# Blocks 2 to 6 are moved between quadrants inside SBUF, so that their sums run on 128x32 tiles

## The chip, the cores and the metric

The kernel runs on one core of a Trainium2 chip. The metric is device microseconds of one execution. Instructions stand in order on each of five engines: PE (matrix multiply), DVE (VectorE), ACT (ScalarE), POOL (GpSimd) and SP, which here only issues DMAs. SBUF has 128 rows (partitions); a quadrant is 32 of them. PE writes into PSUM, whose banks hold 128x512 floats.

## The reference, cut to what matters

```python
# attention between 512 tokens and 32 states, for 8 batches and 8 heads
xread = softmax(scale * x @ state.T) @ state
sread = softmax(scale * state @ x.T) @ x
x = concat([xread, sread], axis=2)              # 8 x (512 + 32) tokens of 512
h = x @ w_in                                    # 512 -> 2048, weights in float64
g = h / (1 + exp(-h))
y = g @ w_out                                   # 2048 -> 512
logits = y @ phi                                # 4352 tokens, 32 slots
d = softmax(logits, axis=tokens);  slot_input = d.T @ y
slot_out[e] = relu(slot_input[e] @ w1[e]) @ w2[e]    # 8 experts, 4 slots each
out = softmax(logits, axis=slots) @ slot_out
```

The kernel never forms y. It makes `w_out @ phi` once (tile `w2p`), takes the logits from g, and sums `d.T @ g` (32 slots by 2048 features) over all tokens. Only that sum is multiplied by w_out.

## The kernel before, in words

Eight blocks of 512 tokens (one batch each) are followed by a block 8 of the 256 state rows. Block k makes g in 16 steps j; step j = 4 fq + i holds features of quarter fq. A step is six full matmuls into a PSUM bank (`h`), an eviction on ACT (or tanh on ACT and a product on DVE for steps 2 to 5) into one of six rotating tiles `g`, and a DVE transpose of 32x32 squares from `g` into the buffer of the block, `blk` (two of these exist; 16x512 floats per partition). The logits (`lg`) of four steps follow as 128x32 matmuls. The weights of a quarter times the states (`wbp`, 64x32 tiles) are made one quarter ahead; their low part is a subtraction on DVE or POOL. Attention for blocks k+1 and k+2 (`sc`, `eT`, `sr`) is woven in.

In block k+1, `s_rep` makes the slot weights of block k: an exponential that writes them four times over (`d`), four PE transposes (`dT`) and one of the logits (`lT`). Then `s_dTg` sums. The DVE transpose works inside each quadrant, so quadrant q holds the tokens of its own 32 features of a step: the sum has to be made of 64 matmuls of 32x32, in four groups of 16 that run side by side, and every group adds to all four PSUM banks. Four DVE instructions then add the banks into `acc`. PE switches form (full, 64x32, 128x32, 32x32) between these kinds of work.

w_out comes as float64 bits in its own order too, half a quarter per block (`wo_block`, at step 10 of blocks 1 to 6, in the buffer of the next block): `conv_nat` makes float32 of it with one ACT and four DVE instructions, and it is stored to DRAM. The last two halves go through `wo_last`.

After block 7, `join7`, block 8 (`hid8`), `fold` (all of `acc` into one bank) and the slots' experts follow. w1 and w2, 32 loads of 1 MB, are loaded into places as these come free (`places`, `load_w`): quarters of the two block buffers, `acc`, the four tiles `win` of w_in, and others. Stores of the output end the program.

The order is not that of the code: a recorder notes each operation with its reads and writes, and a list scheduler picks for each engine the startable operation with the lowest number (place in the code, plus shifts, plus a table `RANK`). SP issues DMAs in one order, with at most eight under way.

Of the kernel before, what the change touches and what calls it, by code (L numbers as in the profile page):

```python
# [15 lines left out]
NB = 8  # L16
# [3 lines left out]
EPS = 1e-9  # L20
# [4 lines left out]
NAT = 10  # L25
# [3 lines left out]
RAW = [("win", 0), ("win", 1), ("wo", 0), ("win", 2), ("wo", 1), ("win", 3), ("wo", 2), ("wo", 3)]  # L29

# [37 lines left out]
    ("0", "ACT", "activation", "acc", 2): -44,  # L68
    ("0", "ACT", "activation", "acc", 3): -519,
    ("0", "ACT", "activation", "acc", 5): 1500,  # L70
    ("0", "ACT", "activation", "acc", 6): 1054,
    ("0", "ACT", "activation", "e", 1): 314,
    ("0", "ACT", "activation", "g", 2): 1009,
    ("0", "ACT", "activation", "g", 12): 347,
    ("0", "ACT", "activation", "part", 7): 723,
    ("0", "ACT", "activation", "s", 1): 373,
    ("0", "ACT", "activation", "win", 1): 190,
    ("0", "ACT", "activation", "win", 4): -1500,
    ("0", "ACT", "activation", "win", 5): -462,
    ("0", "ACT", "copy", "ws", 1): 1500,  # L80
    ("0", "ACT", "copy", "ws", 2): 1246,
    ("0", "DVE", "reduce_max", "asm", 0): -28,
    ("0", "DVE", "reduce_sum", "tm", 1): -405,
    ("0", "DVE", "tensor_scalar", "acc", 4): -317,
    ("0", "DVE", "tensor_scalar", "part", 3): -603,
    ("0", "DVE", "tensor_scalar", "tm", 2): -1193,
    ("0", "DVE", "tensor_scalar", "win", 0): -407,
    ("0", "DVE", "tensor_scalar", "win", 1): -38,
    ("0", "DVE", "tensor_scalar", "win", 4): 1334,
    ("0", "DVE", "tensor_scalar", "win", 5): -7,  # L90
    ("0", "DVE", "tensor_scalar", "win", 6): -1216,
    ("0", "DVE", "tensor_scalar", "win", 7): -1362,
    ("0", "DVE", "tensor_tensor", "s", 5): 1477,
    ("0", "DVE", "tensor_tensor", "wb", 2): 1151,
    ("0", "DVE", "tensor_tensor", "wb", 3): 574,
    ("0", "DVE", "transpose", "blk", 4): -1486,
    ("0", "DVE", "transpose", "blk", 13): 1451,
    ("0", "PE", "matmul", "sc", 2): 865,
    ("0", "PE", "matmul", "sr", 1): 590,
    ("0", "SP", "dma_start", "phi", 0): 1500,  # L100
    ("0", "SP", "dma_start", "raw", 0): 91,
    ("0", "SP", "dma_start", "raw", 2): 189,
    ("0", "SP", "dma_start", "raw", 3): 119,
    ("0", "SP", "dma_start", "raw", 4): 322,
    ("0", "SP", "dma_start", "raw", 5): -2,
    ("0", "SP", "dma_start", "raw", 6): 1174,
    ("0", "SP", "dma_start", "raw", 7): 1292,
    ("0", "SP", "dma_start", "xT", 0): -1080,
    ("0", "SP", "dma_start", "xT", 1): 1386,
    ("7", "ACT", "activation", "m", 0): 1500,  # L110
    ("7", "ACT", "copy", "rd", 0): -1500,
    ("7", "ACT", "copy", "wb", 3): 1125,
    ("7", "ACT", "copy", "wf", 1): 1156,
    ("7", "DVE", "scalar_tensor_tensor", "g", 1): 1500,
    ("7", "DVE", "tensor_scalar", "wo", 1): 1316,
    ("7", "DVE", "transpose", "blk", 2): 1500,
    ("7", "DVE", "transpose", "blk", 4): 1499,
    ("7", "PE", "matmul", "h", 8): 520,
    ("7", "PE", "matmul", "lg", 0): 1057,
    ("7", "PE", "matmul", "lg", 5): 74,  # L120
    ("7", "PE", "matmul", "lg", 12): 313,
    ("7", "PE", "matmul", "wbp", 1): 757,
    ("7", "PE", "transpose", "lT", 0): -377,
    ("8", "DVE", "tensor_copy", "place", 13): 166,
    ("8", "PE", "matmul", "S", 0): 823,
    ("8", "PE", "matmul", "f", 9): -334,
    ("8", "PE", "matmul", "f", 10): -1369,
    ("8", "PE", "matmul", "fold", 0): 1246,
    ("8", "PE", "matmul", "h", 6): -797,
    ("8", "PE", "matmul", "h", 13): 420,  # L130
    ("8", "PE", "matmul", "h", 29): 1217,
    ("8", "PE", "matmul", "lg", 4): 1500,
    ("8", "PE", "matmul", "o", 8): 984,
    ("8", "PE", "matmul", "o", 9): 1121,
    ("8", "PE", "transpose", "dT", 0): 788,
    ("8", "PE", "transpose", "gt", 5): 1212,
    ("m", "ACT", "activation", "e", 0): 695,
    ("m", "ACT", "activation", "e", 1): 1442,
    ("m", "ACT", "activation", "g", 11): -1243,
    ("m", "ACT", "activation", "s", 0): 1500,  # L140
    ("m", "ACT", "copy", "wb", 2): 1453,
    ("m", "ACT", "copy", "wf", 2): -422,
    ("m", "DVE", "reciprocal", "asm", 0): 1500,
    ("m", "DVE", "tensor_scalar", "asm", 0): 1500,
    ("m", "DVE", "tensor_scalar", "blk", 1): -1500,
    ("m", "DVE", "tensor_tensor", "blk", 0): 310,
    ("m", "DVE", "tensor_tensor", "wb", 3): 430,
    ("m", "PE", "matmul", "S", 0): 1500,
    ("m", "PE", "matmul", "h", 4): 505,
    ("m", "PE", "matmul", "h", 6): 1377,  # L150
    ("m", "PE", "matmul", "h", 9): 1448,
    ("m", "PE", "matmul", "lg", 0): 882,
    ("m", "PE", "matmul", "lg", 1): 935,
    ("m", "PE", "matmul", "lg", 4): 1040,
    ("m", "PE", "matmul", "lg", 9): 1500,
    ("m", "PE", "matmul", "sr", 0): 1500,
    ("m", "PE", "matmul", "wbp", 0): 371,
    ("m", "PE", "matmul", "wbp", 1): 775,
    ("m", "PE", "matmul", "wbp", 2): 1500,
    ("m", "PE", "transpose", "eT", 0): 1337,  # L160
# [8 lines left out]
def _runs(ap):  # L169


    dims = list(ap.ap)
    row = dims[0][0]
    if ap.space == bass.MemoryType.DRAM:
        return None
    p0, off = divmod(ap.offset, row) if row else (0, ap.offset)
    quads = 0
    for q in range(p0 // 32, (p0 + dims[0][1] - 1) // 32 + 1):
        quads |= 1 << q
    starts = [off]  # L180
    for step, count in dims[1:-1]:
        starts = [s + step * n for s in starts for n in range(count if step else 1)]
    step, count = dims[-1] if len(dims) > 1 else (1, 1)
# [12 lines left out]
    return quads, even, odd  # L196


class Recorder:
# [90 lines left out]
    def cost(self, op, eng, what, outs, ins, kwargs):  # L290
# [66 lines left out]
        else:  # L357
# [5 lines left out]
            op.cost = 0.42  # L363

# [217 lines left out]
def tile_state_attention_soft_moe(  # L582
# [95 lines left out]
    def conv_nat(raw, dst, pw):  # L678


        v = raw.rearrange("p (c f) b -> p c f b", f=dst.shape[-1])
        lo, hi, d = v[..., 0], v[..., 1], dst.bitcast(U32)
# [987 lines left out]
```

## Time and profile before

| | us |
|---|---|
| runs | 446.56, 447.78, 448.80; median 447.78 |
| the profiled execution | 448.13 |
| its span in the trace | 446.4 |
| PE busy | 420.8 (94%) |
| DVE, ACT, POOL busy | 320.9, 277.0, 99.3 |

The clock granted to PE is full until the last stretch. The span has a start that loads and converts weights (to some 97 us), blocks of 38.4 us each (to some 320 us), and the rest, in which w1 and w2 are loaded. S of block k stands in block k+1. A step's matmul leaves one record in the trace, a matmul in one of the smaller forms two, so that a group of four leaves 8; a few records are missing (a sum's 128 show as 121).

### The profile page before, as it was taken

What the parts mean: (1) busy time and instruction counts of PE and PEld (TensorE: products, weight loads), DVE (VectorE), ACT (ScalarE), POOL (GpSimd) and SP (SyncE); (2) the same over time, 40 slices, a digit from 0 to 9 for tenths busy, and PEclk for the clock granted to TensorE, in tenths of its full rate; (3) what the DMA queues carried; (4) which work ended last, traced back from release to release, by engine and by line L of the source; (5) the groups of instructions that cost most, each with busy time, mean ns of one, the idle gap of its engine ahead of it and who ended that gap; (6) DMA issues with size and microseconds to landing.
All of it is one profiled execution on the core that took longest, in us unless ns stands there. A gap on an engine that the chain in (4) does not pass through costs nothing.

```text
span 446.4 us, 11862 instructions
## 1 busy us (share of the span) xinstructions
PE 420.8 (94%) x5084; PEld 279.5 (63%) x5084; DVE 320.9 (72%) x566; ACT 277.0 (62%) x504; POOL 99.3 (22%) x63
## 2 busy tenths in 40 slices
PE   7889999999999999999999999999999998999970
PEld 5655565766766776676677667667677685334530
DVE  3989999788787976978788697879864654321460
ACT  4899996666775585686668568666746544111360
POOL 0024332152242413224142222421114220000000
PEclk9999999999999999999999999999999999999996
DMA  8999932323402602330370252125297889999997
GB/s 316 423 428 423 329 126 94 97 75 124 135 3 96 236 1 95 133 106 3 96 237 1 96 155 83 18 98 220 101 393 243 305 303 377 402 424 428 399 379 257
DMA packets 23205, 92.19 MB, mean 207 GB/s; under 512 B 1776, under 2 KB 10864, under 8 KB 14832
## 3 DMA queue, kind: packets, MB, share of 16 engines
q1 hardware_dynamic: 23152, 91.43, 55.0%
q8 instruction: 40, 0.66, 0.6%
q14 instruction: 13, 0.11, 0.1%
HBM read 79.37 MB, written 12.06 MB: 205 GB/s over the span
## 4 chain that ended last, share of the span: by engine, by line
PE 85%; DMA 6%; ACT 3%; DVE 2%; issue 1%; SPq 0%; DVEq 0%
PE h L543 43%; PE lg L543 8%; PE S L543 8%; PE wbp L543 6%; DMA xT<-in_xT_dram 5%; PE so L543 3%; PE f L543 3%; PE o L543 2%; PE sc L543 2%; PE eT L543 2%; PE sr L543 1%; DMA ss<-in_stT_dram 1%; DVE acc L543 1%; PE si L543 1%; PE gt L543 1%
## 5 line engine op out<-in xcount | busy, mean ns | idle before, releaser
L543 PE MATMUL h<-ar,wb 128*128 128x512 f32 x768 | 191.2, 401 | 2.7 <-ACT g L543 2.7
L543 PEld LDWEIGHTS h<-ar,wb 128*128 128x128 f32 x768 | 139.4, 188 | 51.7 <-issue 10.9
L543 DVE STREAM_TRANSPOSE blk<-g 128x512 f32<-128x512 f32 x128 | 88.7, 700 | 18.0 <-ACT g L543 17.4
L543 ACT ACTIVATE g<-h 128x512 f32<-128x512 f32 x100 | 59.0, 602 | 52.0 <-PE h L543 43.9
L543 POOL TENSOR_TENSOR wb<-wf,wb 128x512 fp32r<-128x512 f32 x26 | 34.7, 1333 | 83.2 <-PE lg L543 44.8
L543 POOL TENSOR_TENSOR s<-s,tm 128x1024 f32<-128x1024 f32 x12 | 23.3, 1940 | 91.9 <-DVE tm L543 90.3
L543 PE MATMUL S<-blk,dT 32*32 32x512 f32 (+1 forms) x1056 | 37.7, 591 | 0.0
L543 PEld LDWEIGHTS lg<-g,w2p 128*32 128x32 f32 x1056 | 26.9, 109 | 15.8 <-issue 11.5
L543 ACT CAST wb<-wbp 128x512 fp32r<-128x512 f32 x64 | 34.9, 607 | 3.0 <-PE wbp L543 3.0
L543 PE MATMUL lg<-g,w2p 128*32 128x128 f32 (+1 forms) x1056 | 36.6, 279 | 0.0
L543 PE MATMUL wbp<-win,ss 64*32 64x512 f32 x512 | 33.2, 596 | 0.4 <-DVE win L543 0.4
L543 DVE SCALAR_TENSOR_TENSOR acc<-acc,m,S 128x512 f32<-128x512 f32 x28 | 19.1, 743 | 12.3 <-PE S L543 12.3
L543 ACT ACT_TABLE_LOAD x21 | 26.9, 1283 | 1.1 <-PEq L1660 0.7
L543 DVE SCALAR_TENSOR_TENSOR g<-thb,h 128x512 f32<-128x512 f32 x28 | 18.6, 680 | 11.7 <-ACT thb L543 9.5
L543 PEld LDWEIGHTS S<-blk,dT 32*32 32x32 f32 (+1 forms) x1056 | 18.0, 103 | 13.8 <-issue 8.2
L543 DVE TENSOR_TENSOR wb<-wbp,wb 128x512 fp32r<-128x512 f32 x38 | 25.2, 676 | 1.7 <-ACT wb L543 1.4
L543 PE MATMUL h<-wc,rd 128*128 128x512 f32 x96 | 24.2, 402 | 0.0
L543 PE MATMUL lg<-thb 128*128 128x256 f32 x74 | 20.1, 415 | 1.2 <-DVE thb L543 1.2
L543 ACT COPY wf<-wbp 128x512 f32<-128x512 f32 x26 | 15.3, 588 | 7.9 <-PE wbp L543 5.6
L543 ACT ACTIVATE thb<-h 128x512 f32<-128x512 f32 x30 | 17.4, 595 | 4.1 <-PE h L543 3.8
L543 PEld LDWEIGHTS h<-wc,rd 128*128 128x128 f32 x96 | 17.4, 188 | 3.9 <-issue 0.2
L543 DVE TENSOR_REDUCE tm<-s 128x32 f32<-128x1024 f32 (+1 forms) x18 | 19.4, 1078 | 0.3 <-ACT s L543 0.3
(173 smaller groups left out, 576.2 us busy)
## 6 DMA issues: line engine op xcount, KB each, us to landing
place<-in_w_dram SPq DMA_DIRECT2D x17, 1024.0 KB, 7.5
blk<-in_w_dram SPq DMA_DIRECT2D x12, 1024.0 KB, 10.4
xT<-in_xT_dram SPq DMA_DIRECT2D x8, 1024.0 KB, 8.1
raw<-in_w_in_dram SPq DMA_DIRECT2D x8, 1024.0 KB, 14.0
raw<-in_w_outT_dram SPq DMA_DIRECT2D x8, 1024.0 KB, 8.1
xk<-in_xk_dram SPq DMA_DIRECT2D x8, 1024.0 KB, 4.8
blk<-in_w_out_dram SPq DMA_DIRECT2D x6, 1024.0 KB, 4.9
out_dram<-place SPq DMA_DIRECT2D x12, 512.0 KB, 7.7
```

What stands on the lines that cost most here:

```text
L543: made = [call(*args, **kwargs) for call, args, kwargs in op.calls]
```

## The change

The two block buffers get fixed names. `src` receives the transposes and `dst` is what the sum reads. For blocks 2 to 6 (`MOVED`) a quarter of features is moved by four DMAs from `src` to `dst`, inside SBUF: each reads 32 partitions of 8 KB and writes 128 partitions of 2 KB (256 KB), so that all 128 partitions hold tokens. There are 80 such DMAs, on SP. Quarter 0 of a block is moved after the sum of the block before; in blocks 3 to 6 `src` uses two quarters in turn, so the transposes of steps 8 to 11 write where quarter 0 lay. The sum of a moved block is 16 matmuls of 128x32, four per bank, and each bank is added to `acc` when its own four are done. The slot weights are written once, with one transpose, and their sum is multiplied by 4 with one small DVE instruction. Blocks 0, 1 and 7 keep the 32x32 form and write `acc` with a stride.

w_out in its own order goes through `conv`, as w_in does: two ACT instructions, one DVE shift and an integer add on POOL. It is done in the free part of `src`: two halves in block 1, then one each in blocks 3 to 6. `fold` is recorded right after the sum of block 7. Three of the `win` places are filled by four DMAs of 256 KB, each behind the part that it overwrites. The order table `RANK` is new throughout (three of its lines are shown).

```diff
-NAT = 10
+NATS = {1: {9: 0, 13: 1}, 3: {10: 2}, 4: {10: 3}, 5: {10: 4}, 6: {10: 5}}
...
+MOVED = (2, 3, 4, 5, 6)
...
-    ("8", "PE", "matmul", "S", 0): 823,
...
+    ("8", "PE", "matmul", "S", 0): 332,
...
+    ("m", "SP", "dma_start", "dst", 1): 754,
...
+            if outs[0].space == ins[0].space == bass.MemoryType.SB:
+                op.cost, op.bytes = 0.6, 1.5 * b
...
-    def conv_nat(raw, dst, pw):
...
-        nc.scalar.activation(out=dst, in_=hi.bitcast(F32), func=AF.Prelu, scale=2.0**-112, alpha=2.0**32)
-        nc.vector.tensor_scalar(
-            out=pw.bitcast(U32), in0=d, scalar1=3, scalar2=0xFF800000,
-            op0=ALU.logical_shift_left, op1=ALU.bitwise_and,
-        )
-        nc.vector.tensor_scalar(out=d, in0=d, scalar1=3, scalar2=None, op0=ALU.logical_shift_left)
-        nc.vector.scalar_tensor_tensor(out=pw, in0=lo, scalar=2.0**-52, in1=pw, op0=ALU.mult, op1=ALU.mult)
-        nc.vector.tensor_tensor(out=dst, in0=dst, in1=pw, op=ALU.add)
...
-        conv_nat(raw.rearrange("p (f b) -> p f b", b=2), dst, pw)
+        conv(raw.rearrange("p (f b) -> p f b", b=2), dst, pw, None)
...
+    LAST = ("dst", "src") if NB - 1 in MOVED else ("src", "dst")
...
+    def quarter(name, fq):
+        return bufs[name][:, 2048 * fq:2048 * fq + 2048]
+
+    def whole(k):
+
+        t = bufs["dst" if k == 1 else "src"]
+        if k == NB - 1:
+            return t.rearrange("p (y j t) -> p j y t", y=4, j=16)
+        return t.rearrange("p (j y t) -> p j y t", j=16, y=4)
+
+    def at_src(k, fq):
+        return quarter("src", fq if k == MOVED[0] else fq % 2)
+
+    def by_tokens(k, fq):
+
+        for q in range(4):
+            nc.sync.dma_start(
+                out=quarter("dst", fq)[:, 512 * q:512 * q + 512],
+                in_=at_src(k, fq)[32 * q:32 * q + 32].rearrange("r (x n) -> r x n", x=4),
+            )
...
-        if j == 0 and k not in blk_t:
-            new_blk(k)
-        nc.vector.transpose(out=blk_t[k][:, j], in_=g.rearrange("p (y t) -> p y t", y=4))
+        if j == 0 and k < 2:
+            new_blk(("src", "dst")[k])
+        if k in MOVED:
+            nc.vector.transpose(
+                out=at_src(k, fq).rearrange("p (t i c) -> p t i c", t=16, i=4)[:, :, i],
+                in_=g.rearrange("p (t r) -> p t r", t=16),
+            )
+            if i == 3 and fq:
+                by_tokens(k, fq)
+        else:
+            nc.vector.transpose(out=whole(k)[:, j], in_=g.rearrange("p (y t) -> p y t", y=4))
...
+        v = lg[:, 0:128].rearrange("p (y r) -> p y r", y=4)
+        if k in MOVED:
+            to = d = d[:, 0].rearrange("p q r -> p (q r)")
+            to = to.rearrange("p (r y) -> p y r", y=4)
+        else:
+            to, v = d, v.unsqueeze(2).to_broadcast(list(d.shape))
...
+        if k in MOVED:
+            nc.tensor.transpose(p[:, 0:128], d, ident)
+            nc.scalar.copy(out=dT[:, 0:128], in_=p[:, 0:128])
...
+            if k in MOVED:
+                nc.vector.tensor_scalar(out=m[:, 2:3], in0=m[:, 2:3], scalar1=4.0, scalar2=None, op0=ALU.mult)
...
+        def add(i):
+            o, v = acc[:, i], p[i]
+            if k not in MOVED:
+                o = acc.rearrange("p f (q n) -> p f q n", q=4)[:, :, i]
+                v = v.rearrange("p (f n) -> p f n", f=4)
+            if first:
+                nc.vector.tensor_copy(out=o, in_=v)
+            else:
+                nc.vector.scalar_tensor_tensor(out=o, in0=o, scalar=m[:, 3:4], in1=v, op0=ALU.mult, op1=ALU.add)
...
+        for fq in range(4):
+            v = quarter("dst", fq).rearrange("p (q n) -> p q n", q=4)
             with nc.together():
-                for q in range(4):
-                    for x in range(4):
+                for y in range(4):
+                    op = mm(
+                        p[fq][32 * y:32 * y + 32, :], lhsT=dT[:, 32 * y:32 * y + 32],
+                        rhs=v[:, :, 128 * y:128 * y + 128], start=True, stop=True,
+                    )
+            add(fq)
...
+    places = [(LAST[1], 2), (LAST[1], 3), "ss", "at", "A", ("w", 0), (LAST[0], 0), (LAST[0], 1), (LAST[0], 2), ("w", 1)]
+    places += ["g", ("w", 2), "acc", ("w", 3), "wb", "wb", "A", "x", (LAST[1], 0), (LAST[0], 3), "xT", "xk", "at", (LAST[1], 1)]
+    PIECES = (('w', 1), ('w', 2), ('w', 3))
...
+                if nxt_w[0] < len(places) and places[at_p] in PIECES:
+                    for x in range(4):
+                        nc.sync.dma_start(out=wt[kind, i][x], in_=src[:, 512 * x:512 * x + 512])
+                else:
+                    nc.sync.dma_start(out=t, in_=src)
...
                     s_dTg(k - 1)
+                    if k in MOVED:
+                        by_tokens(k, 0)
                     if k == NB - 1:
-                        new_blk(NB)
                         load_w(2)
...
-            if 1 <= k <= 6 and j == NAT:
-                wo_block(k - 1, k + 1)
+            if k in NATS and j in NATS[k]:
+                wo_block(NATS[k][j])
...
             s_dTg(NB - 1)
+            accX = fold()
...
-            accX = fold()
```

On PE, around the sum of block 3 (in block 4). Before (dT is the transposed slot weight, h4_7 step 7 of block 4, blk3 the buffer):

```order
L543 MATMUL dT3_417<-cst_66,d3_415 128x128 x4
...
L543 MATMUL h4_7_444<-ar4_374,wb17_420 128x512 x6
L543 MATMUL lg4_432<-g4_0_410,w2p_68 32x128 x4
...
L543 MATMUL lg4_432<-g4_4_429,w2p_68 32x128 x4
L543 MATMUL S3_0_0_439<-blk3_312,dT3_416 32x512 x4
L543 MATMUL S3_0_1_440<-blk3_312,dT3_416 32x512 x4
L543 MATMUL S3_1_0_441<-blk3_312,dT3_416 32x512 x4
L543 MATMUL S3_1_1_442<-blk3_312,dT3_416 32x512 x4
L543 MATMUL S3_0_0_439<-blk3_312,dT3_416 32x512 x4
...
L543 MATMUL S3_1_1_442<-blk3_312,dT3_416 32x512 x4
L543 MATMUL h4_8_447<-ar4_374,wb18_433 128x512 x6
```

After (dst the tokens of block 3, wbp19 the next weights):

```order
L579 MATMUL dT3_414<-cst_66,d3_412 128x128
...
L579 MATMUL lg4_429<-g4_4_426,w2p_68 32x128 x4
L579 MATMUL h4_6_434<-ar4_372,wb17_417 128x512 x6
L579 MATMUL h4_7_441<-ar4_372,wb17_417 128x512 x6
L579 MATMUL lT3_415<-cst_66,ls3_411 128x128
L579 MATMUL S3_0_0_436<-dst_186,dT3_413 32x512 x4
L579 MATMUL S3_0_1_437<-dst_186,dT3_413 32x512 x4
L579 MATMUL S3_1_0_438<-dst_186,dT3_413 32x512 x4
L579 MATMUL S3_1_1_439<-dst_186,dT3_413 32x512 x4
L579 MATMUL wbp19_0_0_450<-win3_81,ss_67 32x512 x4
L579 MATMUL wbp19_0_1_451<-win3_81,ss_67 32x512 x4
L579 MATMUL h4_8_444<-ar4_372,wb18_430 128x512 x6
```

The four groups of 16 became four groups of four, one to a bank. The logits stand before h4_6 instead of beside the sum, and wbp19 follows the sum.

On DVE, what follows the sum of block 3. Before:

```order
L543 STREAM_TRANSPOSE blk4_387<-g4_7_445 128x512
L543 SCALAR_TENSOR_TENSOR acc_69<-acc_69,m3_413,S3_0_0_439 128x512
L543 SCALAR_TENSOR_TENSOR acc_69<-acc_69,m3_413,S3_0_1_440 128x512
L543 SCALAR_TENSOR_TENSOR acc_69<-acc_69,m3_413,S3_1_0_441 128x512
L543 SCALAR_TENSOR_TENSOR acc_69<-acc_69,m3_413,S3_1_1_442 128x512
L543 STREAM_TRANSPOSE blk4_387<-g4_8_448 128x512
L543 STREAM_TRANSPOSE blk4_387<-g4_9_451 128x512
L543 TENSOR_SCALAR blk5_462<-blk5_462 128x1024
```

After (src is where quarter 0 of block 4 lay):

```order
L579 SCALAR_TENSOR_TENSOR acc_69<-acc_69,m3_410,S3_0_0_436 128x512
L579 SCALAR_TENSOR_TENSOR acc_69<-acc_69,m3_410,S3_0_1_437 128x512
L579 TENSOR_SCALAR tm5_400<-tm5_400 128x32
L579 STREAM_TRANSPOSE src_114<-g4_6_435 128x16x32
L579 SCALAR_TENSOR_TENSOR acc_69<-acc_69,m3_410,S3_1_0_438 128x512
L579 SCALAR_TENSOR_TENSOR acc_69<-acc_69,m3_410,S3_1_1_439 128x512
L579 TENSOR_TENSOR wb19_449<-wbp19_0_0_450,wb19_449 128x512
L579 STREAM_TRANSPOSE src_114<-g4_7_442 128x16x32
...
L579 STREAM_TRANSPOSE src_114<-g4_8_445 128x16x32
L579 STREAM_TRANSPOSE src_114<-g4_9_448 128x16x32
L579 STREAM_TRANSPOSE s5_398<-s5_398 128x1024
...
L579 TENSOR_TENSOR wb20_465<-wbp20_0_0_466,wb20_465 128x512
```

The transpose of g4_8, the first that overwrites quarter 0, stands behind the four adds and seven other instructions; behind it stand more transposes and the low part wb20.

On SP, from the load of batch 6's xT to that of batch 7 (xk is the other layout of x, wo_f32 the DRAM copy of w_out). Before:

```order
L543 DMA xT6_404<-in_xT_dram 128x2048
L543 DMA wo_f32_82<-blk4_387 128x1024
L543 DMA blk5_462<-in_w_out_dram 128x2x1024
L543 DMA xk6_459<-in_xk_dram 128x2048
L543 DMA xT7_479<-in_xT_dram 128x2048
```

After (dst from src are the moves):

```order
L579 DMA xT6_401<-in_xT_dram 128x2048
L579 DMA dst_186<-src_114 128x1x512 x4
L579 DMA src_114<-in_w_out_dram 128x2x1024
L579 DMA wo_f32_82<-src_114 128x1024
L579 DMA xk5_382<-in_xk_dram 128x2048
L579 DMA dst_186<-src_114 128x1x512 x2
L579 DMA wo_f32_82<-src_114 128x1024
L579 DMA dst_186<-src_114 128x1x512 x6
L579 DMA xT7_475<-in_xT_dram 128x2048
```

The loads of xk and xT, and the w_out stores, now stand between moves in the same queue.

## Rows read from the trace of the kernel before

**Rows 1.** The page: busy us (share of the span) and instructions of each engine.

```profile
PE 420.8 (94%) x5084; PEld 279.5 (63%) x5084; DVE 320.9 (72%) x566; ACT 277.0 (62%) x504; POOL 99.3 (22%) x63
```

**Rows 2.** Windows, two blocks: length, PE PEld DVE ACT POOL busy, clock, DMA, GB/s.

```profile
130.00:168.35 38.35, 38.35 (x521) 26.59 (x527) 31.23 (x54) 26.11 (x50) 11.35 (x8) 1.00 0.28 98
245.20:283.60 38.40, 38.40 (x524) 26.65 (x536) 31.18 (x54) 26.15 (x50) 11.40 (x8) 1.00 0.29 98
```

**Rows 3.** Chain of waits, one block: start us, us, engine, tile, instructions.

```profile
235.66 1.01 PE lg L543 x32
236.67 1.02 PE wbp L543 x16
237.69 2.96 PE h L543 x12
240.65 0.44 PE dT L543 x4
241.09 1.38 PE h L543 x6
242.47 0.11 PE lT L543
242.58 1.39 PE h L543 x6
243.97 1.23 PE lg L543 x40
245.20 4.39 PE S L543 x121
```

**Rows 4.** Chain of waits, an earlier block: what follows what.

```profile
138.20 2.77 PE h L543 x12
...
145.61 1.02 PE sc L543 x16
146.63 0.86 PE wbp L543 x16
```

**Rows 5.** Chain of waits after the blocks.

```profile
373.48 1.00 PE fold L543 x8
...
387.39 9.58 PE f L543 x88
...
397.55 1.85 PE f L543 x16
...
435.23 0.40 DVE place L543
```

**Rows 6.** DMA issues: KB each, median us from issue to landing.

```profile
raw<-in_w_in_dram SPq DMA_DIRECT2D x8, 1024.0 KB, 14.0
...
xk<-in_xk_dram SPq DMA_DIRECT2D x8, 1024.0 KB, 4.8
```

**Rows 7.** Groups of instructions: busy us, mean ns of one, idle before.

```profile
L543 DVE STREAM_TRANSPOSE blk<-g 128x512 f32<-128x512 f32 x128 | 88.7, 700 | 18.0 <-ACT g L543 17.4
...
L543 ACT ACTIVATE part<-raw,ulps 128x1024 uint32<-128x1024 uint32 x10 | 12.7, 1274 | 0.4 <-DMA raw<-in_w_in_dram 0.4
...
L543 DVE TENSOR_TENSOR blk<-blk 128x1024 f32<-128x1024 f32 x6 | 11.5, 1910 | 0.0
...
L543 POOL TENSOR_TENSOR acc<-acc,part 128x1024 uint32<-128x1024 uint32 x4 | 9.5, 2387 | 24.6 <-ACT part L543 16.4 <-DVE acc L543 8.2
```

**Rows 8.** Windows after the blocks, columns as before.

```profile
364.00:366.00 2.00, 2.00 (x12) 1.70 (x11) 1.38 (x2) 1.14 (x3) 0.00 (x0) 1.00 0.66 279
366.00:368.00 2.00, 2.00 (x10) 1.63 (x9) 0.00 (x0) 0.00 (x0) 0.00 (x0) 1.00 0.48 94
376.00:387.00 11.00, 9.30 (x143) 4.51 (x143) 5.69 (x23) 2.57 (x8) 0.00 (x0) 1.00 1.00 393
387.00:435.60 48.60, 44.92 (x552) 20.64 (x551) 17.70 (x45) 14.49 (x42) 0.00 (x0) 1.00 1.03 409
```

**Rows 9.** Chain of waits at the start.

```profile
12.80 21.07 DMA xT<-in_xT_dram
```

More of the change, by code (lines that the diff above doesn't have):

```diff
@@ L79 @@
[L79 to L89, printed above, removed]
@@ L101 @@
[L101 to L111, printed above, removed]
@@ L112 @@
[L112 to L123, printed above, removed]
@@ L136 @@
[L136 to L146, printed above, removed]
@@ L159 @@
-    ("m", "PE", "matmul", "wbp", 2): 1500,
-    ("m", "PE", "transpose", "eT", 0): 1337,
+    ("0", "ACT", "activation", "acc", 2): -476,
+    ("0", "ACT", "activation", "acc", 3): -114,
+    ("0", "ACT", "activation", "e", 1): 583,
+    ("0", "ACT", "activation", "g", 1): 536,
+    ("0", "ACT", "activation", "win", 1): -511,
+    ("0", "ACT", "activation", "win", 3): -139,
+    ("0", "ACT", "copy", "e", 0): 325,
+    ("0", "ACT", "copy", "e", 6): 246,
+    ("0", "ACT", "copy", "e", 7): -48,
+    ("0", "ACT", "copy", "wb", 3): 459,
@@ new lines @@
+    ("0", "PE", "matmul", "lg", 8): 500,
+    ("0", "PE", "matmul", "sr", 1): 1500,
+    ("0", "PE", "transpose", "eT", 2): 480,
+    ("0", "SP", "dma_start", "phi", 0): 1500,
+    ("0", "SP", "dma_start", "raw", 2): 1457,
+    ("0", "SP", "dma_start", "raw", 3): 1472,
+    ("0", "SP", "dma_start", "raw", 5): 1493,
+    ("0", "SP", "dma_start", "raw", 6): 1500,
+    ("0", "SP", "dma_start", "ss", 1): 1500,
+    ("0", "SP", "dma_start", "xT", 0): -170,
+    ("7", "ACT", "activation", "m", 0): 450,
@@ new lines @@
+    ("7", "ACT", "copy", "rd", 0): -1064,
+    ("7", "ACT", "copy", "wb", 2): -1069,
+    ("7", "DVE", "tensor_tensor", "wc", 0): 929,
+    ("7", "PE", "matmul", "h", 8): 1304,
+    ("7", "PE", "matmul", "lg", 0): 1500,
+    ("7", "PE", "matmul", "lg", 12): 1066,
+    ("7", "PE", "matmul", "wbp", 1): 1493,
+    ("7", "PE", "matmul", "wbp", 2): 1353,
+    ("8", "ACT", "copy", "dst", 0): -422,
+    ("8", "ACT", "copy", "dst", 1): -430,
+    ("8", "DVE", "reciprocal", "cm", 1): -480,
+    ("8", "DVE", "tensor_copy", "thb", 1): -739,
@@ new lines @@
+    ("8", "PE", "matmul", "lg", 4): 939,
+    ("8", "PE", "matmul", "o", 5): 239,
+    ("8", "PE", "matmul", "o", 7): 385,
+    ("8", "PE", "matmul", "o", 10): 397,
+    ("8", "PE", "matmul", "so", 23): -263,
+    ("8", "PE", "matmul", "so", 24): 553,
+    ("8", "PE", "transpose", "dT", 0): 130,
+    ("m", "ACT", "activation", "e", 0): 1437,
+    ("m", "ACT", "activation", "e", 1): 1272,
+    ("m", "ACT", "activation", "g", 6): 1491,
+    ("m", "ACT", "activation", "sums", 0): 1322,
+    ("m", "ACT", "activation", "thb", 2): 1080,
@@ new lines, in s_dTg @@
+            return p
+        first = sx.pop((k, "first"))
+        def add(i):
[5 more added lines that the diff above has]
+                nc.vector.tensor_copy(out=o, in_=v)
+            else:
+                nc.vector.scalar_tensor_tensor(out=o, in0=o, scalar=m[:, 3:4], in1=v, op0=ALU.mult, op1=ALU.add)
+        if k not in MOVED:
+            blk = whole(k)
+            for y in range(nt):
+                with nc.together():
+                    for q in range(4):
+                        for x in range(4):
+                            t = 4 * y + x
+                            op = mm(
+                                p[q][32 * x:32 * x + 32, :],
+                                lhsT=dT[32 * q:32 * q + 32, 32 * t:32 * t + 32],
+                                rhs=blk[32 * q:32 * q + 32, :, y, 32 * x:32 * x + 32],
+                                start=(y == 0),
+                                stop=(y == nt - 1),
+                            )
+                if k == NB - 1 and y == 0:
+                    nc.after(op, hid8_last[0])
+            for q in range(4):
+                add(q)
+            return
```

220 lines of the change are left out of this document (113 added, 107 removed).

## The prediction

> **What bounds the kernel now.** First the page: PE is busy 94% of the span, the next engine, DVE, 72% [rows 1]. An average says little, so the windows come next. The four blocks between 130 and 283.6 us take 38.4 us each, PE is busy in all of it at full clock, and the 16 DMA engines are busy 0.28 to 0.29 (the first and the last of the four are shown) [rows 2]. Then the chain of waits, to see whether "busy" hides waiting. One block is on it as PE work only, without an entry for a wait: a sum takes 4.39, a step of six matmuls 1.38 to 1.39, a group of logits 0.22 (five take 1.23, four 1.01) [rows 3]. I added up a whole block from such pieces (16 steps, 16 groups of logits, four wbp, sc, sr, transposes, sum, switches) and came to 38.3. So in the blocks nothing but PE counts, and work taken from DVE or ACT is worth nothing there.
>
> After the blocks PE and DMA are both near full: 376 to 387 us has DMA 1.00, 387 to 435.6 has PE 44.9 of 48.6 and DMA 1.03 [rows 8]. The last output leaves DVE at 435.6 [rows 5], and the span ends at 446.4: stores that are still queued.
>
> **The change part by part.** The sum is made against the profiled execution, 448.13 (span 446.4 and 1.7 around it); the median of the runs is 0.35 lower.
>
> *The sum S.* It took 4.39 in 32x32 form, the switch into it included [rows 3]. A group of four 128x32 matmuls with 512 columns is in the trace as f: 88 records are 11 groups in 9.58, 0.87 each; 16 records, two groups, took 1.85, 0.925 each; fold alone, one group with its switch, 1.00 [rows 5]. Four groups at 0.87 are 3.48, so 0.91 is saved per sum, and with five sums (blocks 2 to 6) 4.55. Bounds: 0.925 gives 3.4, 1.00 gives 1.95. I take 0.87, since f runs its groups back to back as S does.
>
> *Transposes of the slot weights.* Four take 0.44, one (lT) 0.11 [rows 3]: 0.33 saved, five times, 1.65.
>
> *Switches of PE's form.* The new order splits work that stood together: the sum stood beside logits, now the logits often stand before h4_6 and wbp follows the sum. Counted through the order by kind (full, 64x32, 128x32; the entry into a 32x32 sum is in its 4.39), there are 116 switches before and 133 after, 17 more. Their price: twelve matmuls of h take 2.96 after wbp and 2.77 after full work, 0.19; sc, the first of its form, takes 1.02 and wbp, as large and of the same form, right behind it 0.86, 0.16; logits 1.01 less four groups of 0.22, 0.13 [rows 3, 4]. At 0.16 they cost 2.7; bounds 2.2 and 3.4. This is the step that eats half the gain.
>
> *The moves.* Each quarter (1 MB) is four DMAs of 256 KB. No transfer inside SBUF is in the trace. The nearest row is xk, 1 MB that is mostly alone, 4.8 from issue to landing; the slowest is raw, 14.0, one of many queued together [rows 6]. I take 6 (near xk, with three further issues); ends 4.8 and 14.0. What waits: the transpose of g4_8 must not write before quarter 0 has left src, and the move starts when the first group of the sum has read dst. In DVE's new order four adds and seven other instructions stand between, some 6 us in any case. Behind that transpose stand two more, a transpose of s5, the norm of the logits and wb20, 4.7 us of DVE, and wb20 is needed by the first step of the next block. From the first group of S to that step PE has 20.7 us of work (three groups, three wbp, sc, seven groups of logits, eight steps, two eT, at the prices above). So a move may take about 16 before PE waits; both ends lie below, and I cost it at nothing. The ring of six g tiles and the two banks of h give no earlier wait. For quarter 3, from step 15 to S is about 16 of PE work. On SP xk, xT and the w_out stores are queued behind moves that wait; xk and xT are used a block later, so they hold nobody.
>
> *w_out's own order.* DVE loses among others an add of 1.91, POOL gets one of 2.39, ACT another pass of 1.27 [rows 7], eight times. In a block of 38.4, DVE works 31, ACT 26, POOL 11 [rows 2]: POOL and ACT have room, and PE waits for none. Nothing; if POOL were late with the low parts of wb it would show as h waiting for wb. The strided writes of acc (blocks 0, 1, 7) and the small multiplication by 4 cost under 1 us of DVE, hidden in the same way.
>
> *fold and places.* fold is the same work earlier; acc is free for its load. The DMA engines stood partly idle from 364 to 368: 2 x 0.34 + 2 x 0.52 = 1.7 us of DMA time [rows 8]. If loads in pieces fill that, the backlog of stores at the end shrinks by as much. I take 1.0; bounds 0 and 1.7, since stores still wait for PE's results.
>
> *The start.* xT of batch 1, on which the chain stands from 12.80 to 33.87 [rows 9], comes two 1 MB loads earlier, up to 5 us at 2.5 each (1.05 MB at 409 GB/s [rows 8]). But what follows it is conversions, whose number is the same; both orders hold 38 dummy matmuls for idle PE time there. I take 0, with 2.5 to either side (half of 5).
>
> Sum: 4.55 + 1.65 - 2.7 + 1.0 = 4.5 saved: 443.6 for a profiled execution, **443.3** against the median.
>
> **The rivals.**
>
> *A. The moves become the bound: slower.* In a block the DMA engines have 0.285 x 38.4 = 10.9 us of work for 3.8 MB [rows 2]. Four quarters more must fit into 37.7 - 10.9 = 26.8, so 6.7 us of all engines each. Above that the sum of a block waits for its tokens, and each 0.1 us costs 4 quarters x 5 blocks x 0.1 = 2 us. It decides (over 0.5% slower) from 7.0; at 7.3 the time is 455. For it: a move reads only a quarter of the partitions, which nothing in the trace does for so many bytes. Against it: existing loads take 10.9 / 3.8 = 2.9 us of the engines per MB. Between 2.9 and the 14.0 of raw, nearer to the first: chance 0.13. The Trainium skill ("SBUF — State Buffer", Door 1: The DMA port swizzle) says that partitions 0 to 31 reach 8 of 16 ports, and gives 189 GB/s for 1 MiB from them; by that, an estimate, a quarter takes 5.5 us and a block's DMA 33 of 37.7 us, no loss but little room. No run so far shows it.
>
> *B. The form gains little.* If four 128x32 groups in this kernel cost as fold did, 1.00 each, S saves 1.95 in all, and the sum is 1.95 + 1.65 - 2.7 + 1.0 = 1.9: 445.9, within 0.5%. For it: only f shows less. Against it: f is 11 groups long. Chance 0.08. The Trainium skill ("TensorE: Matmul & The Clock Gate", Part 3: Packing small matmuls) has a rule of this kind: a pack takes one matmul's time plus about 4 ns per further tile, so 16 tiles would cost only 12 x 4 = 48 ns more than four. At two passes per matmul that is 0.4 per sum, 1.9 in all, the same 445.9; the rows (4.39 / 4 against 0.87) differ with it.
>
> *C. The end belongs to DMA.* DMA is full from 376 on, so if its loads don't start earlier, PE's gain is lost in the queue of stores: 446.5 to 448. For it: 10.8 us of stores after PE's end. Against it: loads start as places come free, and those are freed by PE and DVE, which come earlier. Chance 0.12.
>
> *D. More than forecast*: start and end both give (2.5 and 0.7 more, fewer waits): 438 to 440. Chance 0.07.
>
> **How the numbers follow.** The forecast has 0.60. Its own range: low 443.3 less 2.5 (start), 0.7 (end), 0.5 (switches): 439.5; high 443.3 plus 2.5, 1.0, 0.7 and 1.1 (f at 0.925): 448.5. What a measurement of this kernel can tell from no change is about 0.5%, 2.2 us: faster is below 445.5, slower above 450.0. Of the forecast 0.52 lies below 445.5 and 0.08 above; with D, 0.07, faster is 0.59. Same: 0.08 and B and C, less a little of C, 0.27. Slower: A and a little, 0.14. The range takes in the forecast's own, a part of D, and A up to 7.0 per quarter: 438.5 to 450.5.
>
> **What would show it.** In the chain after, S of a moved block takes 3.5 to 3.7 and dT 0.11; the blocks from the sum of block 2 to that of block 5 take 37.5 to 37.8 each, without waits of PE. The quarter's last DMA lands 5 to 8 us after its first issue, and DMA share in the blocks is 0.55 to 0.8. The sum of block 6 starts some 2 us earlier, and the last result leaves DVE at about 432. What would make it wrong: blocks of 38.4 or more; PE waiting for DMA at S or for DVE wb at h; a DMA share near 1 within the blocks (A); S near 4 (B); an unchanged end with an earlier PE (C).

## The result, and the profile after

The changed kernel takes 450.97 us (median of six runs, 450.25 to 452.15), the kernel before 447.25 beside it: a ratio of 1.0083, with a 95% interval of 1.0061 to 1.0106. It is slower, where 443.3 was forecast, and lies just above the range. The profiled execution took 450.75 (span 448.9). PE is as full as before on the page [rows 1]:

```profile
PE 421.6 (94%) x4573; PEld 274.3 (61%) x4573; DVE 295.4 (66%) x547; ACT 285.7 (64%) x512; POOL 119.6 (27%) x71
```

Two blocks as windows, from one sum to the next (columns as in [rows 2]: length, PE, PEld, DVE, ACT, POOL busy, clock, DMA, GB/s):

```profile
212.73:250.20 37.47, 37.47 (x415) 25.04 (x419) 28.27 (x53) 25.92 (x51) 14.05 (x9) 1.00 0.64 183
250.20:287.69 37.49, 37.49 (x416) 25.04 (x419) 28.50 (x51) 24.99 (x48) 11.44 (x7) 1.00 0.60 170
```

These blocks are what the prediction described: 37.5 us each in place of 38.4, PE busy throughout, the DMA engines 0.60 to 0.64 busy. The chain of waits of the second answers to [rows 3]: the sum takes 3.57 for 4.39, dT 0.11 for 0.44.

```profile
281.88 1.38 PE h L579 x6
283.26 0.11 PE dT L579
283.37 1.23 PE lg L579 x40
284.60 1.58 PE h L579 x6
286.19 0.11 PE lT L579
286.30 1.39 PE h L579 x6
287.69 3.57 PE S L579 x32
```

So the loss lies elsewhere. Sums 0 to 6 stand behind the same number of steps in both orders (24, 40, 56, ... 120), so their starts in the chains can be set against each other (sum 2 of the changed kernel, 168.70, is not on its chain and comes from the trace, counted in the same way). Sum 7 stands three steps earlier in the changed order (132 for 135), so the next common point is `fold`, with 144 steps before it in each. The third column is an experiment that is told below.

| stretch, us | before | after | e1_hold |
|---|---|---|---|
| start to sum 0 | 92.25 | 89.19 | 89.81 |
| sum 0 to sum 2 | 76.10 | 79.51 | 77.86 |
| sum 2 to sum 3 | 38.36 | 44.03 | 37.73 |
| sum 3 to fold | 166.77 | 162.47 | 163.83 |
| fold to the end | 72.92 | 73.70 | 72.17 |
| span | 446.4 | 448.9 | 441.4 |

One block, from sum 2 to sum 3, is 5.7 us longer than before. Its part of the chain, with the steps that the argument needs (start us, us, what):

```profile
171.10 6.31 DMA src<-in_w_out_dram
177.41 0.02 issue
...
177.50 1.22 ACT src L579
178.72 0.48 ACT g L579
...
186.98 10.55 DMA wo_f<-src
...
197.61 0.04 ACT src L579
197.66 0.98 issue
198.63 0.60 ACT g L579
199.23 0.04 issue
199.27 2.93 PE h L579 x6
```

In a block that held nothing but PE work before stand a load of w_out, a store of w_out, and ACT. PE's step at 199.27 waits for an eviction `g`; that stands in ACT's order behind the first conversion instruction of the next half of w_out, which may not overwrite its place in `src` until the store of the half before has landed, 10.55 us after its issue. The waits between 95 and 215 us say the same (engine, line, waited for: us in total, times, longest): first what PE waits for, then a row of ACT's waits.

```profile
PE h L579 <- ACT g L579: 5.7, 3, 3.4
```

```profile
ACT src L579 <- DMA wo_f<-src: 6.2, 2, 3.8
```

After the longest of these waits, 3.4 us, the granted clock is lower too: the step at 199.27 takes 2.93, where a step behind another form of work takes 1.59 later in the block. After the wait of 2.0 us at 112 us it is not: the next four steps take 5.77. Windows around the long wait and at the end:

```profile
187.00:200.00 13.00, 9.58 (x102) 6.27 (x83) 6.62 (x10) 8.47 (x15) 2.59 (x2) 0.96 0.91 313
200.00:212.00 12.00, 12.00 (x183) 8.60 (x181) 9.20 (x19) 9.64 (x19) 4.57 (x3) 0.90 0.67 226
380.00:385.00 5.00, 5.00 (x80) 1.28 (x70) 3.17 (x14) 1.53 (x4) 0.00 (x0) 0.67 0.97 370
```

The last row is the other visible loss. The sum of block 8 takes 3.33 us (1.85 in the held kernel below) in a window with a mean clock of 0.67, that is, mostly at the lower level of 1.2 GHz:

```profile
375.20 0.99 PE fold L579 x8
...
380.50 3.33 PE S L579 x16
```

The transfers (KB each, median us from issue to landing) [rows 6]:

```profile
dst<-src SPq DMA_DIRECT2D x80, 256.0 KB, 4.5
...
src<-in_w_out_dram SPq DMA_DIRECT2D x6, 1024.0 KB, 5.4
...
wo_f<-src SPq DMA_DIRECT2D x6, 512.0 KB, 5.8
```

In the kernel before such a store took 8.8 in the median:

```profile
wo_f<-blk SPq DMA_DIRECT2D x6, 512.0 KB, 8.8
```

It was no faster there; no engine waited for it, because each half lay in another block's buffer, a block apart. In the changed kernel all six halves use one place, and the scheduler drew halves 2 to 5 together: their loads are issued at 162.66, 171.10, 186.35 and 200.38.

### The profile page after: what moved, and what is told of

Same layout as the page of the kernel before. It is cut to its first block, busy times and chain, and to the rows that moved or that the text cites. A ratio compares the mean times of both kernels' runs of the same rounds, so it can differ in the third digit from the quotient of the medians.

```text
span 448.9 us, 10999 instructions
## 1 busy us (share of the span) xinstructions
PE 421.6 (94%) x4573; PEld 274.3 (61%) x4573; DVE 295.4 (66%) x547; ACT 285.7 (64%) x512; POOL 119.6 (27%) x71
## 4 chain that ended last, share of the span: by engine, by line
PE 72%; DMA 12%; ACT 7%; DVE 4%; issue 2%; POOL 1%; SPq 0%; DVEq 0%; ACTq 0%; POOLq 0%
PE h L579 38%; PE S L579 7%; PE lg L579 6%; PE wbp L579 5%; DMA wo_f<-src 4%; DMA raw<-in_w_in_dram 4%; PE so L579 3%; PE f L579 3%; DMA src<-in_w_out_dram 2%; PE o L579 2%; PE eT L579 1%; PE sr L579 1%; ACT g L579 1%; DMA ss<-in_stT_dram 1%; ACT e L579 1%
## 5 line engine op out<-in xcount | busy, mean ns | idle before, releaser
L579 DVE STREAM_TRANSPOSE src<-g 128x512 f32<-128x512 f32 x112 | 76.3, 697 | 27.7 <-ACT g L579 21.3
L579 PE MATMUL wbp<-win,ss 64*32 64x512 f32 x512 | 34.1, 600 | 1.4 <-DVE win L579 1.3
L579 PE MATMUL S<-dst,dT 128*32 128x512 f32 (+1 forms) x296 | 24.8, 609 | 0.0
L579 POOL TENSOR_TENSOR src<-src 128x1024 uint32<-128x1024 uint32 x6 | 14.3, 2391 | 22.1 <-DVE src L579 11.5
L579 PEld LDWEIGHTS lg<-thb 128*128 128x128 f32 x72 | 14.0, 205 | 6.5 <-issue 3.4
```

The source lines that it names most:

```text
L579: made = [call(*args, **kwargs) for call, args, kwargs in op.calls]
```

## The experiments

Theory W: ACT, in order, holds a conversion whose transfer has not landed, and the evictions queue behind it. Rivals: M and A, the moves load the DMA engines or SP; I, the integer adds and ACT's second pass cost time; P, it is the plan as a whole, which changes with every edit, since the scheduler starts anew; C, the half clock at the end. Each run's ratio is to the kernel before, timed on the same chip.

### The halves held in their own blocks

```
+            nc.after(op, held[0])        # op: a half's first ACT instruction
...
+                held[0] = silus[k, j]    # the eviction of the step beside which it is listed
                 wo_block(NATS[k][j])
```

> The changed kernel, with w_out's six halves held in their own blocks: each half's first ACT instruction may not stand ahead of the eviction of the hidden tile beside which the program lists it (block 1 tiles 9 and 13, then tile 10 of blocks 3 to 6). Theory W (the loss is ACT waiting, in order, for the store of the half before, since all halves use one place, and four of them were drawn together into 162 to 216 us): the waits of PE on g at 172 and 196 us go (0.75 and 3.42 us), the half clock of the six-matmul hidden group after them too (1.3 us); the wait at 112 us stays, since the two halves of block 1 stand as before: 444 to 446 us. Rival M (the moves load the DMA queues and SP, and hold everything up by that): no change, 450 to 452. Rival I (the integer adds and the second ACT pass cost it): no change, 450 to 452. Rival C (the half clock of the 128x512 sum after 380 us): 449 to 451.

Measured: 443.5 us, ratio 0.9912 (0.9881 to 0.9943). All that the changed kernel lost came back, and the time is that of the forecast; the wait at 112 us shrank as well (to 0.35 us), which had not been expected. The moves and the integer form are still in it, so M and I are out as the main cause. The chain shows sums and fold at full clock. From sum to sum it has 37.7, 37.5 and then 38.9 us; the last holds a wait of PE of 1.2 us for `srs` of the state softmax:

```profile
167.67 3.57 PE S L579 x32
...
205.40 3.57 PE S L579 x32
...
242.94 3.57 PE S L579 x32
...
281.85 3.57 PE S L579 x32
...
369.23 0.99 PE fold L579 x8
...
374.30 1.85 PE S L579 x16
```

In e11_both_held the half's second ACT instruction is held in the same way.

> The held kernel with both of a half's ACT instructions held in their block (in e1_hold only the first was). Theory W: no conversion waits for its load, 441.5 to 444 us, as the held kernel or a little better. Rival P: anything from 441 to 457, with no waits of ACT on w_out's transfers to go with it.

Measured: 444.52 us, 0.9911 (0.9891 to 0.9931), half a us above the range expected. Between 95 and 350 us ACT waits for a transfer of w_out once, 1.5 us. Against P this is weak, since both kernels have new plans. So the next keeps the plan:

```
+        for n in range(1, 6):            # w_out's halves 1 to 5, after schedule()
+            move([p], [later(0)])        # the two ACT instructions
...
+            move([store], [later(4)])
+            if 1 < n < 5: move([own[n + 1][2][0]], [store])    # the next half's load
```

> The changed kernel with its own order of instructions kept on every engine, but for w_out's halves 1 to 5: the second half of block 1 is put behind the eviction of that block's tile 14, halves 2 to 5 behind the eviction of tile 10 of blocks 3 to 6, each load behind the store of the half before, so that it lands a block ahead. Theory W (ACT, in order, holds a conversion whose transfer has not landed, and the evictions behind it): the waits of PE on g at 112, 172 and 196 us go and the half clock after 199 us with them: 442 to 445.5 us. Rival P (another plan, by chance better or worse, made the difference in the runs before): 449 to 452 us, since the plan is the same.

e10_same_plan is no clear answer: half 2's load was moved too, into columns that block 2 still wrote, so that half was converted from overwritten words. It took 449.39 us, ratio 1.0020 (0.9999 to 1.0040); its profiled execution, the fastest, had no wait of ACT for w_out between 95 and 350 us, but five of PE for `g` there (3.7 us), one for each of halves 1 to 5, whose two ACT instructions stood back to back. e14_same_plan leaves that load where it was and puts an eviction between the two.

> The changed kernel in its own order on every engine, except that the instructions of w_out's halves 1 to 5 stand elsewhere: half 1 behind tile 12 of block 1, halves 2 to 5 behind tile 10 of blocks 3 to 6, one eviction between a half's two ACT instructions, and the loads of halves 3 to 5 behind the store of the half before. Theory W (ACT waits in order for w_out's transfers): the waits of PE at 112, 172 and 196 us go, 443 to 446.5 us (a plan in which no room was left for these instructions beside the later evictions may keep some 1 to 2 us of the loss). Rival P (the plan as a whole, not these waits): 449.5 to 452.

Measured: 446.52 us, 0.9996 (0.9959 to 1.0034; ten executions from 445.12 to 451.84). The interval lies below that of the changed kernel: with every other instruction in its old order, moving these gives back about 0.9%. That is about half of what holding gave back (1.7%). It leaves one wait of ACT for a store, 2.3 us, in block 1, behind which PE waits 1.9 us, and two waits of PE for DVE's products `g`, 1.7 us. From sum 2 to sum 3 it needs 37.80 us. P is out as the main cause. Last, the planner alone:

```
-                end = dma_free + 1.1
+                end = dma_free + 1.1 + (12.0 if "wo_f" in ... else 4.0 if "w_out_" in ... else 0.0)
```

> The changed kernel with one number of its planner changed: a store of w_out's halves counts as landed 12 us later than before, a load of them 4 us later (it had counted such a store as landed under 4 us after its issue, where the trace had 9.06 and 10.55). The program itself then spreads the halves. Theory W: 442.5 to 446.5 us. Rival P: 447 to 457, as the plan falls.

Measured: 444.3 us, 0.9920 (0.9889 to 0.9952). Told that these transfers are slow, the program, otherwise unchanged, spreads the halves by itself, and between 95 and 350 us ACT waits for no transfer of `src`.

### Two places in turn

```
-        dst, pw = (t[:, x:x + 1024] ... for x in (5120, 4096))
+        x = 4096 + 1024 * (n % 2)        # dst in turn; low words converted where they lie in raw
```

> The changed kernel, with w_out's halves landing alternately in two places of the buffer (the low words are converted where they lie, so the columns that held them are the second place); the halves are still drawn forward. Theory W: no half's first ACT instruction waits for the store just before it, so the wait at 112 us goes as well (2.0 us), and of those at 172 to 199 us most (4.4 us and 1.3 of half clock): 443 to 446 us. Rival M (moves): 450 to 452. Rival I (adds and ACT passes, which stay): 450 to 452. Rival C (half clock of the tail): 449 to 451.

Measured: 449.64 us, 1.0038 (1.0007 to 1.0070). A miss: no conversion waits for a store any more, but ACT waits 8.5 us for loads, because raw is now read until the half's last instruction and the next load starts that much later.

> The held kernel (e1_hold: w_out's halves in their own blocks) with the two landing places of e2_two added. Theory W, sharpened by e2_two (there the wait moved from the store to the load, which then had to wait for the half before; it is the drawing together of the halves that costs, not the one place): no difference from the held kernel, 443 to 444.5 us. Rival (the one place costs by itself): faster than it by 1 us or more, 441 to 442.5.

Measured: 456.9 us, 1.0165 (1.0097 to 1.0232), 13 us from what I expected. Only the first of a half's ACT instructions was held; the second reads raw and was planned ahead of the load's landing, in the block before. ACT's waits from 95 to 350 us, then the chain at one of them:

```profile
ACT src L579 <- DMA src<-in_w_out_dram: 11.7, 4, 4.1
```

```profile
231.70 9.62 DMA src<-in_w_out_dram
241.32 0.02 issue
241.34 1.19 ACT src L579
```

> e5_two_held with both of a half's ACT instructions held. There the second, not held, stood ahead of the landing of its load (four waits, 11.7 us). Theory W: that loss goes, and two places or one make no difference once nothing waits: within 1.5 us of e11_both_held, 441.5 to 445 us. Rival (the low words read where they lie, or the other place, cost it): stays at 452 to 457.

Measured: 448.55 us, 1.0009 (0.9984 to 1.0035). Holding the second instruction gives back 8 us, but not to within 1.5 of e11_both_held: one wait for a load is left in block 1 (3.5 us of ACT, 2.6 of PE), PE waits 0.8 us for a move, and the sum of block 8 ran at half clock in the profile (3.53). So the loss comes with either transfer, load or store; what these runs have in common is that ACT's instruction stands ahead of its landing.

### Which arithmetic

```
-        conv(raw..., dst, pw, None)
+        conv_nat(raw..., dst, pw)        # e3, e9; the reverse in e4
```

The rest of each kernel is scaled for its own form, so w_out comes out halved in e3_float and e9_float_held and doubled in e4_before_int.

> The changed kernel with w_out's halves in the arithmetic of before (one ACT instruction and four on DVE, in place of two on ACT, one on DVE and one on POOL), in the one place of the changed kernel. Theory W: the first ACT instruction still waits for the store of the half before, so the loss stays: 449 to 452 us. Rival I (the integer adds and ACT's second pass cost it): 444 to 446. Rival M (moves): 450 to 452.

> The held kernel with w_out's halves in the floating arithmetic of before (one ACT and four DVE instructions for two ACT, one DVE and one POOL; its results are half those of the reference, since the rest of the kernel is left as it is). Theory W: which engine converts is hidden by PE once the halves are spaced, 443 to 445 us. Rival I, for which the 2.3 us that e4_before_int lost speak: the integer adds cost about that here too, so 441 to 442.

Measured: e3_float 455.09 us, 1.0171 (1.0129 to 1.0214); e9_float_held 456.56, 1.0177 (1.0124 to 1.0230). Worse, also when held, with 4.2 and 1.5 us of waits of ACT on transfers. In the chain of e9_float_held the four DVE instructions of a half stand between those of the state softmax (`s`, `tm`, `srs`), and PE waits 5.2 us for `srs`:

```profile
165.07 1.14 ACT src L579
166.21 0.02 issue
166.23 0.69 DVE src L579
166.92 0.62 DVE s L579
167.54 0.57 DVE src L579
...
168.74 1.11 DVE src L579
...
169.92 1.18 DVE src L579
...
172.83 0.46 PE srT L579
...
174.97 6.06 PE S L579 x32
```

The sum behind that wait runs at the lower clock (6.06 for 3.57). The integer form, which e1_hold keeps, is therefore not what made the changed kernel slow; with this table of priorities, made for it, it is much the better one.

> The kernel before, with nothing but the integer arithmetic of the changed kernel for w_out's halves, each still in its own block's buffer: Theory W: no difference, 446.5 to 448.5 us. Rival I: slower by 2 us or more, 449.5 to 452.

Measured: 449.73 us, 1.0049 (1.0031 to 1.0067). A miss, and taken alone in favour of I. The profile loses 2.1 us between sum 0 and sum 2 (78.15 for 76.10), of which 1.0 is a wait of PE's dT for the exponential `d`. In the rest PE does not wait. Its order came out anew, with a table of priorities that was made for the other arithmetic: from sum 0 to sum 2 it changes form 26 times, where the kernel before does so 18 times (counted in the traces; entries into 32x32 left out). Eight changes at the prediction's 0.13 would make up 1.0, an estimate; but the next three stretches of this run, with two changes more each, are at most 0.1 us longer than before, and no run separates the order from the second ACT pass, so this part stays open. From sum 0 to sum 2 the held kernel also loses 1.8, with 24 changes and 0.35 of waits.

### More to move

```
+            if q < 2:                    # two of a quarter's four pieces a second time, to DRAM
+                op.calls.append((call, args, dict(out=more[k - 2, fq, q]..., in_=v)))
```

> The held kernel with half again as many bytes moved: of the four pieces of each moved quarter, two are also written to a scratch tensor in DRAM (nothing reads it). The prediction's cover (a quarter's move took 6 us, and PE waits from 16 us on): the share of the DMA engines in blocks 2 to 6 rises from 0.70 to about 0.87 and the time stays, 443 to 445 us. Rival A (the moves are at the edge of what the DMA engines can carry): PE waits on the moves, 447 to 455 us.

> e11_both_held with half again as many bytes moved, as in e6_more_moves. Theory W: of the 36 us that e6_more_moves lost, what ACT waited for w_out's transfers (24.5 us in blocks 1 to 6, and the half clock behind it) goes: 444 to 455 us. Rival A (the moves themselves, which DVE and the sums wait for, are at their edge): 465 us or more.

Measured: 479.48 us, 1.0682 (1.0611 to 1.0754), and with both instructions held 471.16, 1.0506 (1.0460 to 1.0553). The smaller losses that I expected failed in both, and rival A, dead at the size of the change, is alive at half again the bytes. Whether it is the bytes, the number of DMAs (120 for 80) or their place in the one queue was not tried. In e6_more_moves ACT waits 16.3 us for loads of w_out; take that away and the wait is DVE's, in e13_more_both, for the moves themselves (PE in turn waits 17.4 us for DVE's products `g`). ACT's row in the first, then DVE's in the second:

```profile
ACT src L579 <- DMA src<-in_w_out_dram: 16.3, 4, 6.4
```

```profile
DVE src L579 <- DMA dst<-src: 48.5, 11, 9.9
```

The chain of e13_more_both shows the place: a load of 1 MB and the move behind it take 19.6 us together, while the DMA engines are 0.74 to 0.84 busy in windows of the blocks, so not full.

```profile
226.47 8.94 DMA src<-in_w_out_dram
235.43 10.61 DMA dst<-src
246.07 0.05 DVEq L579
246.26 0.09 DVE src L579
```

### The end and the start

```
-            accX = fold()                # e7: back to its place behind sum7()
-    PIECES = (('w', 1), ('w', 2), ('w', 3))
+    PIECES = ()
```

> The held kernel with the end of the kernel before: the fold of acc where it stood, and the places behind win loaded whole. The prediction's term for these two (1.0 us): 444 to 445.5 us. Rival (the end is set by the transfers anyway): 443 to 444, no difference.

Measured: 444.5 us, 0.9930 (0.9903 to 0.9957). The interval overlaps that of e1_hold, and from fold to the end the two profiles need 72.24 and 72.17 us. The gain of 1.0 is not shown; what the held kernel gains there on the kernel before (72.92) has another cause. On PE the fold has the same neighbours in all three orders, so its new place in the program moved nothing there. Ahead of four groups of the output's matmuls PE waits 1.4 us in the kernel before and 0.7 in both held ones, which is nearly the whole difference.

> e1_hold with the priorities of the kernel before for the start (the part of the table for block 0 and what stands ahead of it). If the start's gain hangs on them, the sum of block 0 starts near 92 us instead of 89.8, and the time is 445.5 to 447.5 us; if it comes of the rest of the change, 443 to 445 us.

Measured: 449.04 us, 1.0034 (1.0011 to 1.0057), 5.5 above the held kernel. In its profile (span 445.6, the fastest execution) sum 0 starts near 91.5, not 92, and a further 2.1 us are lost up to sum 2. The start's gain hangs on the new table, and more than expected.

### The clock at the end

```
-FILL = ((0.0, 60.0),)
+FILL = ((0.0, 60.0), (365.0, 365.6))     # two idle matmuls between the two dT groups of block 8
```

> The changed kernel with two idle matmuls of 128x256 (their results are not read) between the two dT groups of the end, where PE waits 0.75 us ahead of the sum that ran at half clock. Rival C (the half clock of the end, 1.4 us in the sum and some 0.2 in siT): if PE is kept at it the clock stays, 449 to 449.6 us; if the clock falls all the same, 450.5 to 451.5. Theory W: no more than that 1.6 us can come of it, not below 449.

> e1_hold (443.5 us, full clock at the last sum in its profile) with the two idle matmuls of e16_tail_fill: if idle of PE there brings the half clock in some executions, 442.5 to 443.5 us, with less spread than the 2.8 us of e1_hold; if it has nothing to do with it, 443.2 to 444.2 (the two matmuls take 0.86 us where 0.75 are idle).

> e15_planner (444.3 us, half clock at the last sum in its profile, 3.44 us in place of 1.85) with the same two matmuls: full clock there and 442.3 to 443.5 us if the idle brings the half clock; 444 to 445 if not.

Measured: 450.08 us, 1.0051 (1.0026 to 1.0077), ten executions from 447.78 to 453.1; 445.16, 0.9924 (0.9898 to 0.9949); 443.82, 0.9902 (0.9885 to 0.9918). None of the three medians lies in one of its expected ranges: the first and the third lie between two, the second above both. All three profiles have full clock in that sum. The changed kernel gains 0.9 us on its median, the planner's version 0.5, the held one loses 1.7; the intervals overlap each time, so in the median no more than about 1 us was to be had there, and the cause of the half clock stays open. e20_planner_fill and e1_hold are the fastest, and not to be told apart.

## Why the prediction was wrong

**The step that failed is "w_out's own order ... POOL and ACT have room, and PE waits for none. Nothing."** The room was there: ACT works 26 of 38.4 us in [rows 2] and 25 to 26 after. But a share of busy time does not say whether an instruction can start. It stands in order, its start hangs on a transfer, and what is behind it is `g`, which PE needs for its steps of 1.4 us. The change added such waits, with the buffer shared by all halves, and I priced only the work. The paragraph on the moves has "the w_out stores ... queued behind moves that wait" and "they hold nobody", with a reason for xk and xT alone; the stores hold the next half. From sum 2 to sum 3 the price is 6.3 us (44.03 against 37.73 with the halves held): 4.4 of waiting at 172, 181 and 196 us, 1.35 of half clock in the step behind, 0.5 not assigned. Nor did any rival name this; A, the one on the slower side, had the moves themselves, which in the changed kernel hold PE's matmuls nowhere.

Could it have been seen? Most of it. In the changed order the conversions of four halves stand close together on ACT, and the profile before has the store at 8.8 us. I followed the order around the sums alone.

**The sum and dT.** 3.57 for the 3.48 taken: 0.82 saved and not 0.91. f was the right row, and B is dead. The pack rule of the Trainium skill ("TensorE: Matmul & The Clock Gate", Part 3: Packing small matmuls), weighed there, would have made it 0.4. dT gave its 0.33.

**The blocks.** Forecast: 4.55 + 1.65 - 2.7 = 3.5 less. From sum 0 to fold the held kernel is 1.8 shorter than the kernel before: 1.76 longer up to sum 2, 3.57 shorter behind it (201.56 for 205.13). Five sums at 0.82 and five dT at 0.33 save 5.75. Against that stand 1.5 of PE's waits (0.35 in block 1, 1.2 for `srs`) and 0.44 for four transposes eT, which the kernel before makes ahead of sum 0. About 2.0 is left for the switches and whatever else changed. The traces have 16 more of them in this stretch (78 for 62; 17 in the whole span, as counted), so 0.12 each where 0.16 was taken; they were not measured apart. The bounds of that term are not consistent: 17 at 0.19 are 3.2, not 3.4. The ends of the forecast's own range, 439.5 and 448.5, add up to 439.6 and 448.6.

**The moves.** Near enough at their size: the last of a quarter's four DMAs lands 7.3 us in the median after the first is issued (6.9 to 9.6; one DMA 4.5), where 6 was taken and 5 to 8 expected; DMA 0.60 to 0.64, no wait of PE in the two blocks shown. The 16 us of cover are not refuted (at 19.6, in e13_more_both, PE waits), but there a load of w_out ahead of a move uses up half of them, and that load was not in the working. A block of the held kernel, with its half of w_out, shows what a quarter costs the engines:

```profile
205.40:242.94 37.54, 37.54 (x415) 25.04 (x419) 28.28 (x52) 27.01 (x50) 13.80 (x8) 1.00 0.72 211
```

0.72 x 37.5 = 27.0 us, less the 10.9 of before, over four quarters: 4.0 each, where A decides from 7.0. The rule of the Trainium skill ("SBUF — State Buffer", Door 1: The DMA port swizzle) had given 5.5, so it is on the safe side of what this block shows.

**The end.** Forecast 1.0, of fold and places; measured 0.75 in the held kernel, but e7_old_end has it too. Near in size, wrong in cause, and 1.5 us of half clock ate it in the changed kernel.

**The start.** Taken as 0 with 2.5 to either side; sum 0 came 3.06 earlier (2.44 in the held kernel), of which 0.44 are the four eT that now stand behind it. The stretch up to sum 2 gave it back: halves 0 and 1 are both converted in block 1, and PE waits there 2.0 us at 112 us for the same reason.

With the waits for w_out nearly removed the time is 443.5 us, in e1_hold, against 443.3 forecast. That it is so close is partly luck. In the profiles the held kernel gains 5.0 where 4.5 was forecast, but by other terms: 2.4 at the start for 0, 1.8 from sum 0 to fold for 3.5, 0.75 at the end for 1.0.

## What to carry to other kernels

When a change lets several transfers share one buffer, write down for each in-order engine the first instruction that touches it again, what lands last before it, and what is queued behind; the engine's idle share answers none of these. Take the landing time from the slowest such transfer in the trace, not from the planner's number: a scheduler that counts a transfer as landed too early puts its user at the head of the queue. And a wait of PE can cost more than its length: here 3.4 us of waiting were followed by 1.35 more at the lower clock.

## What was not expected of the hardware

The half clock of the last sum does not follow from the program's order there. In e11_both_held and e15_planner the same instructions stand in front of it, behind the same idle of PE, at the same instants of the span (siT at 374.68, the sum at 375.13 in both); the first ran the sum at full clock, the second mostly at the lower level. The sum's row in the first, then in the second:

```profile
375.13 1.85 PE S L579 x16
```

```profile
375.13 3.44 PE S L579 x16
```

Moves inside SBUF that read 32 partitions and write 128 cost the DMA engines 4.0 us per quarter of 1 MB, an estimate from the held kernel's block above, where the other transfers of a block cost 2.9 per MB. That left them room here. Half again as many bytes cost 27 us (471.16 against 444.52), though the DMA engines were not full.
